# Weights in long contiguous runs, a row-wise MLP and an output tail in four column groups, in a decode block on one core

## Chip, cores, metric

One core of one Trainium2 chip. The metric is device time in microseconds (us) of one execution. "Span" is the time of one profiled execution, about 1.8 us shorter than the device time of the same run.

## The reference, cut

```python
def reference(A_x, A_k_cache, A_v_cache, A_wq, A_wo, B_x, B_w1, B_b1, B_w2, B_b2):
    xn = _layernorm(A_x)                                    # A_x: (8, 1, 640) bf16
    # attention: q = xn @ wq, 32 heads of 128, caches (8, 32, 4096, 128)
    # p = softmax(q k^T / sqrt(128)); o = p v; a = o @ wo    wq (640, 4096), wo (4096, 640)
    # MLP: m = gelu(_layernorm(xn) @ w1 + b1) @ w2 + b2      w1 (640, 1728), w2 (1728, 640)
    return A_x + a + m
```

The two caches are 268 MB each; with the weights the kernel reads 552 MB and does little arithmetic on each byte. This is a streaming problem.

## The kernel before

The caches are cut into 64 tiles (8 batches, 8 groups of 4 heads). A tile is 4.2 MB of K and 4.2 MB of V, with 32 KB runs on each of 128 partitions. There are two K buffers and two V buffers. VectorE computes three quarters of the scores of a tile (two rounds of multiply, add, reduce) and TensorE one quarter (transposes, then matmuls); TensorE multiplies with V.

All loads are issued by SyncE, in the order of a position number, and it waits in that order: a load that may not be issued yet holds back those behind it.

```python
        def kpieces(t):
            return [(0, NJ)]
        ...                                                       # cut
        for t in range(T):
            pos = (-100.0, -94.0)[t] if t < NK else t - 1.5       # K tile t
            ...
            pos = t + 0.6                                         # V tile t
            R = (["wqBfree"], ["wqBfree", "wqAfree", "ovfree"])[t] if t < NV else []
            ...
```

The weights wq and w1 lie in the space of the V buffers until V is loaded. Their rows were spread over partitions as "(c k) n -> k c n", so each partition got five separate rows:

```python
        ld(-99.0, wqa_sb, A_wq[:, 0:QP * P].rearrange("(c k) n -> k c n", k=P), ["wqA"], "wqa")       # 1 KB runs
        ld(-93.0, wqb_sb, A_wq[:, QP * P:H * P].rearrange("(c k) n -> k c n", k=P), ["wqB"], "wqb")   # 7 KB runs
        ld(-95.2, w1_sb, B_w1.rearrange("(c k) f -> k c f", k=P), ["ovw1"], "w1")                     # 3456 B runs
        ld(-95.1, w2_sb[:, 0:FC - 1, :], B_w2[0:(FC - 1) * P, :].rearrange("(c k) n -> k c n", k=P), ["ovw2a"], "w2a")   # 1280 B
```

Only four heads of wq (0.66 MB, 640 KB) are loaded at first, so that the first tiles can start; the other 28 come after K1. The last steps put the output together:

```python
                    for a in range(HT):
                        for k in range(2):
                            r = e.matmul(TRF[0:B, k, 0:D // 2], oTn_sb[:, a, :],
                                         wo_sb[:, a, k * D // 2:(k + 1) * D // 2], start=False, ...)
```

## Time and profile before

| | before |
|---|---|
| device time, first 3 runs | 1297.64 us (1297.46 to 1299.62) |
| span of the profiled run | 1297.0 us |
| bytes moved | 552 MB, mean 426 GB/s |
| VectorE busy | 1119.4 us (86%) |
| VectorE's first multiply starts | 19.15 us |
| last V data landed | 1290.99 us |

First the page of the kernel before: three rows of its 40 equal slices, 32.4 us each. PEclk and DMA are in tenths, GB/s is what the DMA engines moved.

```profile
PEclk9555565555555555555555655556655565555556
DMA  9999999999999999999999999999999999999997
GB/s 383 399 425 433 431 429 434 426 434 432 428 435 425 436 434 428 432 425 436 434 431 431 425 435 435 431 429 431 429 435 431 429 431 429 436 430 426 433 430 302
```

DMA is at 9 (90% or more) in every slice but the last, and from the third slice to the last but one near 430 GB/s. So DMA bounds this kernel, and any change must either move fewer bytes, or touch the two ends.

The chain of waits of the kernel before, from the middle of the run: start, length, what.

```profile
330.16 35.17 DMA KV_sb<-in_A_v_cache_dram
365.38 3.62 PE PV_ps L619 x32
369.01 35.17 DMA KV_sb<-in_A_v_cache_dram
404.22 3.62 PE PV_ps L619 x26
```

The chain alternates between a landing of V (L619 is the product with V, which starts when V is there) and the next issue. The chain goes through every second V tile, so from 365.38 to 404.22 us two K tiles and two V tiles have moved: 16.8 MB in 38.84 us, 432 GB/s. At that rate, 552 MB take 1278 us. The rest, 19 us, is at the ends and in the small loads.

The loads that SyncE issued, in order of time (start, length, engine and line, operation, what; x2 is two merged):

```profile
0.74 0.39 SPq L370 DMA_DIRECT2D KV_sb<-in_A_k_cache_dram  x1
1.19 0.41 SPq L370 DMA_DIRECT2D KV_sb<-in_A_wq_dram  x1
1.65 0.52 SPq L370 DMA_DIRECT2D KV_sb<-in_B_w_dram  x1
2.21 17.41 SPq L370 DMA_DIRECT2D w_sb<-in_B_w_dram  x2
19.67 0.58 SPq L370 DMA_DIRECT2D KV_sb<-in_A_k_cache_dram  x1
20.29 0.43 SPq L370 DMA_DIRECT2D KV_sb<-in_A_wq_dram  x1
...
76.41 0.33 SPq L370 DMA_DIRECT2D KV_sb<-in_A_k_cache_dram  x1
76.78 0.44 SPq L370 DMA_DIRECT2D wo_sb<-in_A_wo_dram  x1
78.02 0.33 SPq L370 DMA_DIRECT2D KV_sb<-in_A_v_cache_dram  x1
93.37 0.33 SPq L370 DMA_DIRECT2D KV_sb<-in_A_k_cache_dram  x1
```

K0, then a part of wq, w1, w2. The two issues of w2 took SyncE 17.4 us (the chain of waits splits them into 8.4 and 9.0), although the view names nothing that they waited for. At 76.41 us K3 was issued, then a wo, V2, and at 93.37 us K4. VectorE's first multiply on a K tile (timeline, VectorE):

```profile
19.15 3.35 DVE L544 TENSOR_TENSOR Y_sb<-KV_sb,qbc_sb 128x6144 bf16<-128x6144 bf16 x1
```

And the end of the chain of waits: the last V piece, the last projection, the output.

```profile
1290.99 0.72 PE PV_ps L629 x32
...
1292.51 2.17 PE TR_ps L669 x8
...
1294.70 0.48 DVE out_sb L749
```

The page's last part gives the median from issue to landing:

```profile
KV_sb<-in_A_k_cache_dram SPq DMA_DIRECT2D x64, 4096.0 KB, 26.8
KV_sb<-in_A_v_cache_dram SPq DMA_DIRECT2D x63, 4096.0 KB, 35.2
```

A V load lands 35.2 us after its issue, but its own transfer is 9.7 us (a quarter of the 38.84 us above): the queue holds more than two loads ahead.

### The profile page before, as it was taken

How to read it: one execution, taken by the hardware profiler on the slowest of the kernel's cores; microseconds unless marked ns; L12 is line 12 of the kernel's file. 1: busy time of each engine (PE TensorE's matmuls, PEld its weight loads, DVE VectorE, ACT ScalarE, POOL GpSimd, SP SyncE). 2: the span in 40 equal slices, each digit the busy share in tenths (PEclk: the TensorE clock that was granted, in tenths of full speed). 3: DMA queues.
4: the chain of work that ended last, by engine and by line, in shares of the span. 5: the costliest groups of instructions: out<-in, count | busy, mean ns of one | idle time of the engine just before them, and what ended most of it. 6: DMA issues, size and time to landing. Idle time of an engine off the chain costs nothing.

```text
span 1297.0 us, 19542 instructions
## 1 busy us (share of the span) xinstructions
PE 657.6 (51%) x7884; PEld 428.4 (33%) x7884; DVE 1119.4 (86%) x574; ACT 493.1 (38%) x1202; POOL 0.2 (0%) x4
## 2 busy tenths in 40 slices
PE   4354554555454455444555445544545544545555
PEld 3233333333233243232333233332332332333332
DVE  7698898898898898888988888988988988988884
ACT  2244344334344244343344343343442443432442
POOL 0000000000000000000000000000000000000000
PEclk9555565555555555555555655556655565555556
DMA  9999999999999999999999999999999999999997
GB/s 383 399 425 433 431 429 434 426 434 432 428 435 425 436 434 428 432 425 436 434 431 431 425 435 435 431 429 431 429 435 431 429 431 429 436 430 426 433 430 302
DMA packets 26738, 552.04 MB, mean 426 GB/s; under 512 B 2313, under 2 KB 8801, under 8 KB 10082
## 3 DMA queue, kind: packets, MB, share of 16 engines
q1 hardware_dynamic: 26688, 551.80, 99.4%
q8 instruction: 10, 0.16, 0.1%
q10 hardware_dynamic: 34, 0.02, 0.0%
q14 instruction: 6, 0.05, 0.0%
HBM read 551.80 MB, written 0.01 MB: 425 GB/s over the span
## 4 chain that ended last, share of the span: by engine, by line
DMA 86%; PE 9%; DVE 2%; SPq 2%; issue 1%; ACT 0%; DVEq 0%
DMA KV_sb<-in_A_v_cache_dram 84%; PE PV_ps L619 8%; DMA KV_sb<-in_A_wq_dram 2%; SPq L370 2%; DVE Y_sb L544 1%; DVE Y_sb L548 0%; PE C_ps L457 0%; PE TR_ps L512 0%; ACT KT_sb L515 0%; PE TR_ps L669 0%; ACT qT_sb L462 0%; ACT S_sb L532 0%; PE PV_ps L629 0%; PE S_ps L522 0%; DVE out_sb L749 0%
## 5 line engine op out<-in xcount | busy, mean ns | idle before, releaser
L544 DVE TENSOR_TENSOR Y_sb<-KV_sb,qbc_sb 128x6144 bf16<-128x6144 bf16 x128 | 429.1, 3352 | 93.9 <-DMA KV_sb<-in_A_k_cache_dram 93.9
L551 DVE TENSOR_REDUCE S_sb<-Y_sb 128x48 f32<-128x3072 bf16 x128 | 429.1, 3353 | 4.4
L515 ACT ACTIVATE KT_sb<-TR_ps 128x1024 bf16<-128x1024 bf16 x256 | 254.8, 1021 | 249.2 <-PE TR_ps L512 247.6
L512 PE MATMUL TR_ps<-ident_bf,KV_sb 128*128 128x128 bf16 x2048 | 249.6, 309 | 102.7 <-DMA KV_sb<-in_A_k_cache_dram 84.2
L619 PE MATMUL PV_ps<-KV_sb,P_sb 128*16 128x512 bf16 x2040 | 224.6, 619 | 130.4 <-DMA KV_sb<-in_A_v_cache_dram 130.4
L512 PEld LDWEIGHTS TR_ps<-ident_bf,KV_sb 128*128 128x128 bf16 x2048 | 201.2, 142 | 115.5 <-DMA KV_sb<-in_A_k_cache_dram 89.2
L548 DVE TENSOR_TENSOR Y_sb<-Y_sb 128x3072 bf16<-128x3072 bf16 x128 | 224.9, 1757 | 4.4
L522 PE MATMUL S_ps<-qk_sb,KT_sb 128*128 128x4 bf16 x2048 | 97.9, 170 | 147.4 <-ACT KT_sb L515 145.8
L638 ACT ACTIVATE E_sb<-PV_ps 128x512 bf16<-128x512 f32 (+1 forms) x65 | 38.5, 592 | 319.8 <-PE PV_ps L619 317.9
L522 PEld LDWEIGHTS S_ps<-qk_sb,KT_sb 128*128 128x128 bf16 x2048 | 86.1, 109 | 178.2 <-ACT KT_sb L515 178.2
L619 PEld LDWEIGHTS PV_ps<-KV_sb,P_sb 128*16 128x16 bf16 x2040 | 63.1, 124 | 242.9 <-DMA KV_sb<-in_A_v_cache_dram 136.0
L583 ACT ACTIVATE P_sb<-S_sb,NB_sb 32x128 bf16<-32x128 f32 x256 | 101.9, 398 | 3.8
L644 PE MATMUL C_ps<-sel_bf,E_sb 128*128 128x4 bf16 x256 | 16.9, 172 | 102.6 <-DVE rinv_sb L600 79.3
L565 PE MATMUL CH_ps<-ident_f,M_sb 128*2 128x128 f32 (+1 forms) x33 | 12.2, 370 | 103.7 <-DVE M_sb L563 103.7
L577 ACT ACTIVATE NB_sb<-CH_ps 128x2 f32<-128x2 f32 (+1 forms) x33 | 5.7, 172 | 152.0 <-PE CH_ps L573 152.0
L532 ACT ACTIVATE S_sb<-S_ps 32x32 f32<-32x32 f32 x256 | 48.2, 188 | 31.5 <-PE S_ps L522 29.2
L644 PEld LDWEIGHTS C_ps<-sel_bf,E_sb 128*128 128x128 bf16 x256 | 11.4, 104 | 134.1 <-DVE rinv_sb L600 79.7
L595 PEld LDWEIGHTS C_ps<-rs_sb,mask_f 128*128 128x128 f32 x256 | 42.7, 252 | 24.1 <-issue 24.1
L583 ACT ACTIVATION_READ_ACCUMULATOR P_sb<-S_sb,NB_sb 32x1 f32 x256 | 47.0, 184 | 0.0
L595 PE MATMUL C_ps<-rs_sb,mask_f 128*128 128x2 f32 x256 | 45.4, 299 | 0.0
L565 PEld LDWEIGHTS CH_ps<-ident_f,M_sb 128*2 128x2 f32 (+1 forms) x33 | 2.6, 80 | 106.6 <-DVE M_sb L563 106.6
L661 DVE TENSOR_TENSOR oTn_sb<-C_ps,rinv_sb 128x8 bf16<-128x8 f32 x32 | 4.7, 147 | 26.8 <-issue 22.5
(82 smaller groups left out, 158.6 us busy)
## 6 DMA issues: line engine op xcount, KB each, us to landing
KV_sb<-in_A_k_cache_dram SPq DMA_DIRECT2D x64, 4096.0 KB, 26.8
KV_sb<-in_A_v_cache_dram SPq DMA_DIRECT2D x63, 4096.0 KB, 35.2
wo_sb<-in_A_wo_dram SPq DMA_DIRECT2D x8, 640.0 KB, 28.0
KV_sb<-in_A_wq_dram SPq DMA_DIRECT2D x1, 4480.0 KB, 28.5
KV_sb<-in_B_w_dram SPq DMA_DIRECT2D x1, 2160.0 KB, 19.2
w_sb<-in_B_w_dram SPq DMA_DIRECT2D x1, 2080.0 KB, 24.3
KV_sb<-in_A_v_cache_dram SPq DMA_DIRECT2D x1, 2048.0 KB, 12.7
KV_sb<-in_A_v_cache_dram SPq DMA_DIRECT2D x2, 1024.0 KB, 15.0
```

Source lines behind the costliest of these rows:

```text
L512: r = e.transpose(TR_ps[:, it.box[0], jj * P:(jj + 1) * P], kv[:, n * BK + jj, :], ident_bf[:, :])
L515: add("act", t - 0.59 + 0.12 * n, lambda e: e.activation(KT_sb[:, m % NS, :, :].rearrange("p a b -> p (a b)"), TR_ps[:, it.box[0], :], ACT ...
L522: r = e.matmul(S_ps[:, c:c + HT], KT_sb[:, m % NS, jj, :], qk_sb[:, :, b % HB], start=True, stop=True)
L532: r = e.activation(S_sb[s, g % SR, i, 0:JP], S_ps[s, 0:JP * HT].rearrange("p (j a) -> p j a", a=HT)[:, :, a], ACT.Copy)
L544: return e.tensor_tensor(y, kv[:, j0:j1, :], qbc_sb[:, g % 2, i, :][:, None, :].to_broadcast([P, nj, P]), ALU.mult)
L548: lambda e, y=y, y2=y2: e.tensor_tensor(y2, y[:, :, 0:P // 2], y[:, :, P // 2:P], ALU.add),
L551: lambda e, y2=y2, j0=j0, j1=j1: e.tensor_reduce(S_sb[:, g % SR, i, j0:j1], y2, AX.X, ALU.add),
L583: r = e.activation(P_sb[s, g % PR, i, :, a, :], S_sb[s, g % SR, i, :].rearrange("p (m c) -> p m c", c=4), ACT.Exp, bias=NB_sb[s, g % 2, i: ...
L595: r = e.matmul(RS_ps[:, a * GT:(a + 1) * GT], mask_f[:, a, :], rs_sb[:, g % PR, :], start=True, stop=True)
L619: r = e.matmul(PV_ps[32 * ct:32 * ct + HT * 4, t % 2, :], P_sb[:, g % PR, i, m, :, :].rearrange("p a c -> p (a c)"), vv[:, 4 * m:4 * m + 4 ...
L638: add("act", pos, lambda e: e.activation(E_sb[:, k, 0:n], PV_ps[:, k, 0:n], ACT.Copy), R=[("PV", k)], W=[("E", k)], X=[("PVb", k)])
L644: r = e.matmul(OT_i, E_sb[:, t % 2, c * P:(c + 1) * P], sel_bf[:, c:HT * 4:4], start=(c == 0), stop=(c == 3 and not last))
```

## The change

It intends to shorten the two ends. The weights get a layout in which each partition holds consecutive rows, so a partition is one contiguous run: 40 KB of wq, 17 KB of w1, 16 KB of w2. The whole wq then comes in one load. The queries and the MLP's hidden layer are computed with activations as rows (8 rows of 512 or 432 columns) and turned by small transposes. TensorE's loop has two tiles instead of four, the row sums take one matmul instead of four, the last sum for the base of the output moves from VectorE to TensorE, and the last projection runs in four column groups side by side.

```diff
-        ld(-99.0, wqa_sb, A_wq[:, 0:QP * P].rearrange("(c k) n -> k c n", k=P), ["wqA"], "wqa")
-        if H > QP:
-            ld(-93.0, wqb_sb, A_wq[:, QP * P:H * P].rearrange("(c k) n -> k c n", k=P), ["wqB"], "wqb")
+        ld(-99.0, wq_sb, A_wq.rearrange("(k c) n -> k c n", c=DC), ["wq"], "wq")
 ... cut
-            pos = (-100.0, -94.0)[t] if t < NK else t - 1.5
+            pos = (-100.0, -98.0)[t] if t < NK else t - 1.5
 ... cut
-            pos = t + 0.6
-            R = (["wqBfree"], ["wqBfree", "wqAfree", "ovfree"])[t] if t < NV else []
+            pos = (0.45, 1.2)[t] if t < NV else t + 0.6
+            R = (["wqfree"], ["wqfree", "w1free", "hfree"])[t] if t < NV else []
 ... cut
-        ld(-95.2, w1_sb, B_w1.rearrange("(c k) f -> k c f", k=P), ["ovw1"], "w1")
-        ld(-95.1, w2_sb[:, 0:FC - 1, :], B_w2[0:(FC - 1) * P, :].rearrange("(c k) n -> k c n", k=P), ["ovw2a"], "w2a")
+        ld(-95.2, w1_sb, B_w1.rearrange("(k c) f -> k c f", c=DC), ["w1"], "w1")
+        ld(-95.1, w2_sb[:, 0:FC, :], B_w2[0:FC * P, :].rearrange("(k c) n -> k c n", c=FC), ["w2"], "w2")
 ... cut: row queries and row MLP
+            for n in range(H * P // 512):       # 8 blocks of 512 columns
+                        for kc in range(DC):
+                            i = e.matmul(TRF[0:B, it.box[0], :], xnT_sb[:, 0, kc, :], wq_sb[:, kc, s],
+                                         start=(kc == 0), stop=(kc == DC - 1))
 ... cut: row sums
-                for a in range(HT):
-                    r = e.matmul(RS_ps[:, a * GT:(a + 1) * GT], mask_f[:, a, :], rs_sb[:, g % PR, :],
-                                 start=True, stop=True)
+            add("pe", rp, lambda e: e.matmul(RS_ps, ones_f[:, :], rs_sb[:, :, :].rearrange("p a g -> p (a g)"),
+                                             start=True, stop=True),
 ... cut: last projection
-                        for k in range(2):
-                            r = e.matmul(TRF[0:B, k, 0:D // 2], oTn_sb[:, a, :],
-                                         wo_sb[:, a, k * D // 2:(k + 1) * D // 2], start=False,
+                        for k in range(4):
+                            r = e.matmul(TRF[32 * k:32 * k + B, 0, 0:D // 4], oTn_sb[:, a, :],
+                                         wo_sb[:, a, k * D // 4:(k + 1) * D // 4], start=False,
```

## The prediction

> What bounds it now. The DMA queue. The page's slices show the 16 engines 99% busy from the third slice to the last but one, at about 431 GB/s; the chain of waits is 84% landings of V tiles. The Trainium skill ("DMA: Bandwidth & Descriptors", section "Where 436 GB/s comes from") gives a fabric ceiling of 435 GB/s, and the trace agrees: in the middle of the run a K tile and a V tile (8.39 MB) land every 38.85 us, 432 GB/s. All 552 MB at 432 GB/s are 1278 us of the 1297 us span. Only 19 us are not at this rate: about 2 us before data flow, a poor stretch in the first 64 us (windows of 4 us: 293 GB/s at 12 to 16 us, 262 at 56 to 60 us), 8 loads of wo (1.75 us each where 1.5 is the full rate), thinning out over the last 5 us, and 6.0 us from the last V landing (1291.0) to the end. VectorE is second: a tile takes 17.0 us, a pair with its softmax 36.8 us (from 64.6 to 101.4 us, timeline), against 38.85 us of DMA.
>
> What changes.
> 1. Longer runs for wq, w1, w2. From the DMA records (an estimate from packet sizes and durations), 1 KB packets move 19.4 B/ns per engine, 1280 B 22.3, 3456 B 24.6, 7 KB 25.9, 32 KB 26.9. At 26.9 the weights (9.7 MB) cost 2.5 us less of all-engine time. This removes the poor stretch at 12 to 16 us, and the issue that sat 17 us on w2.
> 2. But the whole wq (5.2 MB) must land before any query, where 0.64 MB did. Before, VectorE's first multiply started at 19.2 us. Now: K0 and wq land at about 24 us; 40 matmuls of 512 columns, some 9 to 12 us (0.43 us each at half clock, from four concurrent PV matmuls taking 0.43; half that before the throttle, which came some 7 us after PE got busy); 32 small transposes, 2 to 3 us; copies and broadcast 1.7 us. First multiply at about 38 us. Loads queued ahead (wq, K1, w1, w2, V0) keep DMA busy to about 54 us. K2 and V1 should be just in time, but K4 waits for VectorE's last multiply of tile 2, about 48 us after its first multiply: 86 us, when the queue has run dry at 83. I expect a hole of about 4 us there, and after 108 us as many bytes moved as before, within 1 MB. Then VectorE catches up by 1 us a tile.
> 3. Row MLP, row sums in one matmul, two-tile loop, qbc in its own bank: save PE time, which is off the path. Steady state stays 38.85 us a pair.
> 4. Tail: the last projection, 8 matmuls of 320 columns in sequence (2.15 us), becomes 16 of 160 in four column groups, about 0.6 to 0.8 us; outputs in halves cost about the same. Minus 1.4 us, all on the path.
>
> Sum: 1297.6 - 1.4 (tail) - 0.5 (start, -2.5 and the better queue against the hole) = 1295.7 us, range 1290.5 to 1300.5. Faster by over 2%: 0.01; within 2%: 0.98; slower by over 2%: 0.01.
>
> Right if: pair period unchanged at 38.85; first multiply at 36 to 41 us; DMA low in some window between 82 and 90 us; last landing to end 4.4 to 5.0 us.
>
> Wrong if: the queries run faster, or K4's hole is filled (then up to 5 us better); the MLP on PE frees V1 late, or PE is throttled through the queries, VectorE starting at 46 us (up to 8 us worse); or the steady rate shifts.

## The result, and the profile after

| | before | after |
|---|---|---|
| device time, 4 runs each | 1298.63 us (1297.46 to 1301.33) | 1297.93 us (1297.65 to 1299.02) |
| span of the profiled run | 1297.0 us | 1296.1 us |
| VectorE's first multiply | 19.15 us | 39.09 us |
| last V data landed | 1290.99 us | 1290.96 us |
| from there to the end | 6.0 us | 5.1 us |

The ratio is 0.9993, with a 95% interval of 0.9975 to 1.0011: the same. A ratio is the mean time of one kernel's fast runs over that of the other's in the same rounds, so it is not quite the ratio of the medians above.

A large rewrite thus moved the last landing by 0.03 us; below it turns out that two larger terms cancelled there. The page of the kernel after, same rows:

```profile
PEclk9655556555565555556555555555665556655566
DMA  9989999999999999999999999999999999999997
GB/s 405 426 360 431 430 435 430 428 430 432 434 431 430 427 435 434 429 432 425 437 433 428 434 425 436 433 427 436 425 435 432 429 435 426 434 432 428 432 430 330
```

The first two slices are better (405 and 426 against 383 and 399 GB/s). The third is worse: 360 against 425. What was won in 65 us was given back in the next 32, and somewhat more. Part of the gain is not run length: the kernel before had a low place of its own at 56 to 60 us (262 GB/s; 395 after), where V0 was issued only at 56.29 us, when the queries of the other 28 heads had freed the space of wq. The windows of 4 us around that place in the kernel after (busy us of each engine with counts in brackets, granted clock, DMA share, GB/s):

```profile
80.00:84.00 4.00, 1.61 (x28) 1.61 (x29) 3.96 (x3) 3.54 (x10) 0.00 (x0) 0.50 0.85 363
84.00:88.00 4.00, 3.26 (x43) 1.72 (x45) 3.96 (x2) 2.48 (x6) 0.00 (x0) 0.50 0.02 4
88.00:92.00 4.00, 2.24 (x21) 0.80 (x10) 3.96 (x2) 0.60 (x1) 0.00 (x0) 0.50 1.08 393
```

From 84 to 88 us DMA moved 4 GB/s. Windows of 1 us put the hole from 83.3 us (131 GB/s in the 84th us) to 88.0 us: 4.7 us. In the kernel before, the same three windows have 459, 414 and 418 GB/s. The loads that SyncE issued in the kernel after:

```profile
0.74 0.41 SPq L365 DMA_DIRECT2D KV_sb<-in_A_k_cache_dram  x1
1.20 0.41 SPq L365 DMA_DIRECT2D KV_sb<-in_A_wq_dram  x1
1.66 0.42 SPq L365 DMA_DIRECT2D KV_sb<-in_A_k_cache_dram  x1
2.13 0.50 SPq L365 DMA_DIRECT2D KV_sb<-in_B_w_dram  x1
2.67 1.11 SPq L365 DMA_DIRECT2D w_sb<-in_B_w_dram  x2
...
87.30 0.36 SPq L365 DMA_DIRECT2D KV_sb<-in_A_k_cache_dram  x1
89.90 0.34 SPq L365 DMA_DIRECT2D KV_sb<-in_A_v_cache_dram  x1
```

The whole set of weights was now issued by 3.8 us, without the 17 us. But K4 was issued at 87.30 us only, and V2 at 89.90, after 2.0 us more of waiting for the product with V0 to free its buffer. K4 needs the buffer of K2, and VectorE read K2 until 87 us. It was late because it had started late (timeline of the kernel after):

```profile
25.18 10.81 PE L451 MATMUL TR_ps<-KV_sb,xnT_sb 128*8 128x512 bf16 x40 [12.51 <-DMA KV_sb<-in_A_wq_dram]
27.51 0.59 ACT L455 ACTIVATE Y_sb<-TR_ps 8x512 bf16<-8x512 f32 x1 [16.08 <-PE TR_ps L451]
29.55 0.59 ACT L455 ACTIVATE Y_sb<-TR_ps 8x512 bf16<-8x512 f32 x1 [1.45 <-PE TR_ps L451]
30.62 0.59 ACT L455 ACTIVATE Y_sb<-TR_ps 8x512 bf16<-8x512 f32 x1 [0.49 <-PE TR_ps L451]
...
39.09 3.36 DVE L543 TENSOR_TENSOR Y_sb<-KV_sb,qbc_sb 128x6144 bf16<-128x6144 bf16 x1 [25.49 <-ACT qbc_sb L482]
...
83.67 3.35 DVE L543 TENSOR_TENSOR Y_sb<-KV_sb,qbc_sb 128x6144 bf16<-128x6144 bf16 x1
```

wq landed at 25.18 us; the 40 matmuls of the queries took 10.81 us; VectorE started at 39.09. Before, it started at 19.15. The last line is its last multiply on K2: it ends at 87.02, and K4 is issued 0.3 us later.

The copies of the query blocks also show how fast TensorE was: they start at 27.51, 29.55, 30.62 us and then every 1.08 us. The first two blocks (ten matmuls) took about 2.1 us each, 0.43 us per matmul of 512 columns, the others 0.215. The Trainium skill, "TensorE: Matmul & The Clock Gate", Part 1, says that an idle TensorE runs at half rate until about 3.4 us of sustained work have passed; this trace agrees: the rate changed at 29.3 us, 4.1 us after the first of these matmuls.

The steady state of the kernel after, same view as before:

```profile
331.56 35.17 DMA KV_sb<-in_A_v_cache_dram
366.77 3.62 PE PV_ps L615 x29
370.41 35.19 DMA KV_sb<-in_A_v_cache_dram
405.63 3.62 PE PV_ps L615 x30
```

366.77 to 405.63 us is 38.86 us, against 38.84. And the end:

```profile
1290.96 1.12 PE PV_ps L625 x32
...
1292.89 0.73 PE TR_ps L664 x16
...
1293.65 0.31 DVE out_sb L766
```

The last projection took 0.73 us instead of 2.17. The last product with V (L625, L629 before) took 1.12 us instead of 0.72 though; it is the same work at a lower granted clock (the 2 us window from 1290 us on reads 0.50 after, 1.00 before).

The start cost more than the 0.03 us between the last landings show. Summed in windows of 20 us, the kernel after had moved 1.6 MB more than the kernel before at 80 us and 0.7 MB less at 100 us, and it stayed 0.4 to 0.8 MB behind up to 1280 us: on average 0.54 MB, which is 1.25 us at 432 GB/s. It caught up only in the last 10 us of the transfers. The windows there, two of the kernel before and then the same two of the kernel after (the last two numbers are DMA share and GB/s):

```profile
1286.00:1288.00 2.00, 1.41 (x20) 1.27 (x24) 0.21 (x1) 0.53 (x1) 0.00 (x0) 1.00 0.71 291
1288.00:1290.00 2.00, 1.29 (x28) 0.36 (x16) 0.00 (x0) 0.60 (x1) 0.00 (x0) 1.00 0.19 78
1286.00:1288.00 2.00, 1.04 (x16) 0.31 (x16) 0.15 (x1) 0.00 (x0) 0.00 (x0) 1.00 1.02 426
1288.00:1290.00 2.00, 0.80 (x8) 0.11 (x8) 0.00 (x0) 0.60 (x1) 0.00 (x0) 0.70 0.54 217
```

In the kernel before, part of the DMA engines already had nothing left to do from 1286 us on, while the last data landed at 1290.99 all the same. In the kernel after they were full up to 1288 us. Why is open, and there is only one trace of the kernel before. That the two last landings agree is therefore luck: the start lost 1.25 us and the end of the transfers gave it back.

### The profile page after: what moved, and what is told of

Its sections match the earlier page's. It is cut to its first block, busy times and chain, and to the rows that moved or that the text cites. A ratio compares the mean times of both kernels' runs of the same rounds, so it can differ in the third digit from the quotient of the medians.

```text
span 1296.1 us, 19692 instructions
## 1 busy us (share of the span) xinstructions
PE 650.0 (50%) x7853; PEld 408.1 (31%) x7853; DVE 1121.7 (87%) x586; ACT 500.3 (39%) x1241; POOL 0.2 (0%) x4
## 4 chain that ended last, share of the span: by engine, by line
DMA 77%; DVE 10%; PE 9%; issue 3%; ACT 0%; SPq 0%; DVEq 0%
DMA KV_sb<-in_A_v_cache_dram 75%; PE PV_ps L615 7%; DVE Y_sb L543 5%; DVE Y_sb L547 3%; DVE S_sb L550 2%; DMA KV_sb<-in_A_wq_dram 2%; PE TR_ps L451 1%; PE CH_ps L564 0%; DVE M_sb L562 0%; SPq L365 0%; PE PV_ps L625 0%; PE PV_ps L689 0%; PE TR_ps L462 0%; DVE rinv_sb L596 0%; PE TR_ps L664 0%
## 5 line engine op out<-in xcount | busy, mean ns | idle before, releaser
L566 DVE TENSOR_REDUCE M_sb<-CH_ps 2x4 f32<-2x128 f32 (+1 forms) x33 | 9.2, 279 | 15.9 <-PE CH_ps L564 15.9
L675 PE MATMUL ACC_ps<-oTn_sb,wo_sb 128*128 128x8 bf16 x620 | 21.5, 169 | 0.0
## 6 DMA issues: line engine op xcount, KB each, us to landing
w_sb<-in_B_w_dram SPq DMA_DIRECT2D x1, 2080.0 KB, 43.8
```

The source lines that it names most:

```text
L675: r = e.matmul(ACC_ps[:, c * B:(c + 1) * B], wo_sb[:, a, c * P:(c + 1) * P], oTn_sb[:, a, :], start=False, stop=False, skip_group_check=True)
```

## The experiments

My theory: the long runs do save DMA time, but the start is paced by VectorE's first multiply, which now waits for the whole wq and all queries. Two K buffers let VectorE's lateness through to the queue at K4; the queue runs dry at 83.3 us, and everything after K4 is shifted. The rivals: the longer runs give nothing; or all DMA time counts and the change has simply added as much as it removed; or TensorE's work matters.

The runs were made in three calls, on different chips. The kernel before had medians of 1298.32, 1300.77 and 1299.13 us. The new code varied less: the kernel after had 1297.93 and 1298.44. Differences of half a us between runs therefore say little, and the landings in the traces are compared as well as the times. Every result was correct.

### wq_first: wq before K0

```diff
-        ld(-99.0, wq_sb, ...)
+        ld(-100.5, wq_sb, ...)        # K0 is at -100.0
```

> The changed kernel, with only the order of the first two loads turned: wq, then K0. Theory (the gain of the long runs is lost in a hole before K4, because VectorE starts 39.1 us into the span, after the whole wq and the queries): wq lands 9.7 us earlier, VectorE's first multiply comes at about 29.4 us, K4 is issued at about 77.6 us, before the queue runs dry at 83.3 us, so the hole of 4.7 us (83.3 to 88.0 us) is gone and the time falls by 4 to 5 us, to about 1293.3 us, with the steady pair still at 38.85 us. Rival (the longer runs simply give nothing, the first stage is bound by bytes and small costs, and the hole would only move elsewhere): within 1 us of 1297.9 us.

Measured: 1293.18 us (1292.96 to 1293.26, 5 runs), the kernel before beside it 1298.32; ratio 0.9961 (0.9947 to 0.9974). VectorE's first multiply at 30.25 us, last landing at 1285.99. The window in which the hole was, in this run:

```profile
84.00:88.00 4.00, 1.89 (x16) 1.62 (x16) 2.04 (x1) 0.95 (x2) 0.00 (x0) 0.50 0.99 426
```

The hole is gone (K4 was issued at 78.60), and with it 4.75 us of time and 4.97 us at the last landing. The same bytes, the same packets, the same instructions on every engine but SyncE: only two loads changed places. This version beats both kernels, by 0.4%; under the 2% line that still counts as the same.

### wq_third: wq after K1

```diff
-        ld(-99.0, wq_sb, ...)
+        ld(-97.0, wq_sb, ...)         # K1 is at -98.0
```

> The changed kernel with wq after K1 instead of before it. Theory (startup is paced by VectorE's first multiply): first multiply 9.7 us later, at about 48.8 us, K4 issued at about 97 us, all later loads 9.7 us later, time about 1307.6 us. Rival (the DMA queue has slack for this, the total is bytes over rate): no change, 1297.9 us.

Measured: 1307.51 us (1307.15 to 1308.14). First multiply at 48.56 us, 9.47 us later than in the kernel after; time 9.58 us more. One us of start costs one us of total. The rival, that the queue has slack, falls. The time was lost in other places, though: with the queries later, V0 and K2 were issued later too (45.48 and 60.39), and the queue ran low from 44 to 48 us (151 GB/s) and from 56 to 64 us (41 and 250 GB/s) already.

### k4_parts: only K4 in three pieces

```diff
         def kpieces(t):
-            return [(0, NJ)]
+            return [(32, 80), (0, 32), (80, NJ)] if t == 4 else [(0, NJ)]
```

> The changed kernel with the load of K tile 4 alone in three pieces, columns 32 to 80 first, so that a piece can be issued when VectorE's first multiply of tile 2 is over (78.6 us) instead of its second (87.3 us). The loops of the engines then start a few tiles later; the order of operations is the same. Theory: the hole at 83.3 to 88.0 us closes, but K5 is still issued at 104.2 us and the queue now runs dry at about 102.8 us: a new hole of 2 to 3 us there, so the time falls by only about 2 us, to 1296. Rival (a hole is a hole: filling it gives it all back): 4.7 us less, 1293.2. Rival (the hole is unimportant): 1297.9.

Measured: 1295.54 us (1294.97 to 1295.67), 2.4 us less than the kernel after; last landing at 1288.71, 2.25 us earlier. The windows of this run:

```profile
84.00:88.00 4.00, 3.26 (x44) 1.77 (x43) 3.97 (x2) 2.67 (x6) 0.00 (x0) 0.50 0.96 401
...
100.00:104.00 4.00, 2.92 (x32) 0.80 (x24) 4.00 (x2) 0.60 (x1) 0.00 (x0) 0.50 0.80 340
104.00:108.00 4.00, 0.00 (x0) 0.00 (x0) 3.93 (x3) 0.00 (x0) 0.00 (x0) 0.50 0.78 262
```

The hole at 84 us is filled, and a smaller one stands at 100 to 108 us, where 340 and 262 GB/s replace 430: (430 - 340 + 430 - 262) x 4 / 430 = 2.4 us lost. Half of what was filled came back as the next wait, as expected: K5 was still issued at 104.21 us.

### k4to7_parts: K4 to K7 in three pieces

```diff
-            return [(0, NJ)]
+            return [(32, 80), (0, 32), (80, NJ)] if 4 <= t < 8 else [(0, NJ)]
```

> As k4_parts, for K tiles 4 to 7. Theory: K5 and K6 are issued before the queue runs dry too, no hole from 83 us to 130 us, 4 to 5 us less than the changed kernel, about 1293.3 us, although VectorE's first multiply stays at 39.1 us. If VectorE itself bounded the first stage, it would stay at 1296 to 1298.

Measured: 1294.94 us (1293.92 to 1294.98), 3.0 us less than the kernel after, last landing at 1287.63, 3.3 us earlier; its first multiply was at 39.49 us. (The profiled run, 1293.92 us, was the fastest of the five.) The two places where the holes stood:

```profile
84.00:88.00 4.00, 3.26 (x49) 1.98 (x50) 3.96 (x3) 2.81 (x6) 0.00 (x0) 0.50 1.00 418
...
100.00:104.00 4.00, 3.12 (x32) 0.92 (x24) 4.00 (x2) 0.76 (x2) 0.00 (x0) 0.50 0.92 392
```

No 4 us window between 80 and 140 us is below 385 GB/s, so the holes are gone while VectorE's start stayed late. I had expected 4 to 5 us. Part of the rest is the pieces themselves: their packets of 8 and 12 KB moved at 26.1 and 26.3 B/ns per engine against 26.9 for 32 KB, which is about 0.9 us more by the packet durations (512 packets x 9.4 ns and 1024 x 10.1 ns, over 16 engines). The remaining half us I have not followed up.

### short_runs: the packets of before, in the kernel after

```diff
-        ld(-99.0, wq_sb, A_wq.rearrange("(k c) n -> k c n", c=DC), ["wq"], "wq")
+        for a, (n0, n1) in enumerate([(0, 512), (512, H * P)]):
+            ld(-99.0 + 0.01 * a, wq_sb[:, :, n0:n1], A_wq.rearrange(...)[:, :, n0:n1], [("wq", a)], "wq")
+        # w1: one load for each c, 3456 B runs; w2: one load for each c, 1280 B runs
```

> The changed kernel with the packets of the kernel before: wq in 1 KB and 7 KB runs (two loads), w1 in five loads of 3456 B runs, w2 in thirteen of 1280 B runs; same bytes into the same places. The short runs cost about 2.5 us more of all-engine time (from the packet durations: wq 1.0, w1 0.5, w2 1.0). Theory (VectorE paces the start through wq): only wq's part counts, since wq lands 1.0 us later and K4 is issued 1.0 us later; the 1.5 us of w1 and w2 are swallowed by the hole, which shrinks. Time about 1299.0, plus 1.0 us. Rival (every us of DMA time counts): plus 2.5 us, 1300.4. Rival (run length means nothing here): 1297.9.

Measured: 1300.08 us (1299.44 to 1300.73); the kernel before 1300.77. Last landing at 1293.77, 2.81 us later than in the kernel after. First multiply at 41.84, 2.75 us later. So the whole loss again equals the delay of VectorE's start, as the theory says; but my size for it, 1.0 us, was wrong, and on the time alone the rival (2.5 us) did better. wq landed 1.9 us later, not 1.0. By 28 us the DMA had moved 0.3 MB less than in the kernel after by the 4 us windows, 0.4 MB by the packet records, which is 0.7 to 1.0 us at 432 GB/s: no more than the packet durations had said. Why the last piece of wq landed later still was not followed up. The queries took 11.64 us instead of 10.81. This run could not part the theories.

### wq_first_short: the same, without a hole

```diff
 # short_runs, and
-            ld(-99.0 + 0.01 * a, wq_sb[:, :, n0:n1], ...)
+            ld(-100.5 + 0.01 * a, wq_sb[:, :, n0:n1], ...)
```

> As short_runs, on top of wq_first, where there is no hole. Theory: now every us of DMA time counts, so the short runs cost the whole 2.5 us: 1295.7 against 1293.2. Rival (only wq's landing counts, here too): plus 1.0 us, 1294.2.

Measured: 1295.91 us (1295.28 to 1296.11), 2.7 us above wq_first; last landing 3.1 us later, while the first multiply was only 2.1 us later (32.36 against 30.25). SyncE was busy issuing w2 up to 42.86 us, so that V0 was issued at 42.90 instead of 27.18; but no 4 us window from 4 to 92 us is below 347 GB/s, so the queue did not run dry over it. Here more was lost than VectorE's delay: without a hole DMA itself counts.

### short_w1_w2 and wq_first_short_w1_w2: short runs only where wq is not touched

```diff
-        ld(-95.2, w1_sb, B_w1.rearrange("(k c) f -> k c f", c=DC), ["w1"], "w1")
+        for c in range(DC):
+            ld(-95.2 + 0.001 * c, w1_sb[:, c, :], B_w1.rearrange("(k c) f -> k c f", c=DC)[:, c, :], [("w1", c)], "w1")
         # w2 likewise; wq in 40 KB runs, at -99.0 (first) or -100.5 (second kernel)
```

> The changed kernel with wq in long runs, and w1 and w2 alone in the short runs of the kernel before (3456 B and 1280 B). They cost about 1.5 us of all-engine time after wq has landed. Theory (VectorE, started by wq, paces the loads up to K4, and the hole before K4 has room): VectorE's first multiply at 39.1 us as in the changed kernel, hole 1 to 1.5 us shorter at its front, time unchanged within 0.5 us of the changed kernel. Rival (every us of DMA time counts): plus 1.5 us.

> The same short w1 and w2 on top of wq_first, where there is no hole. Theory: here every us of DMA time counts: plus 1.0 to 1.5 us against wq_first's 1293.2, so 1294.2 to 1294.7. Rival (w1 and w2 never matter): 1293.2.

Beside them on the same chip, the kernel after once more:

> The changed kernel itself once more, to stand beside the next two on the same chip (the kernel before ran 1297.6 to 1301.9 us within the last call): 1297.9, within 1 us.

Measured: after_again 1298.44 us (1297.95 to 1298.73), short_w1_w2 1297.97 us (1297.28 to 1298.87), wq_first_short_w1_w2 1293.96 us (1293.91 to 1294.11). In the kernel after, the short runs of w1 and w2 cost nothing: the times overlap, and the last landing moved by 0.44 us with a first multiply 0.34 us later (39.83 against 39.49). The window from 80 to 84 us moved 459 GB/s instead of 369, since the queue ran dry later: the hole took them in. In wq_first they cost 0.8 us of time and 1.0 us of landing, a little less than expected; wq_first itself was timed in another call. So the long runs of w1 and w2 save something like 0.8 us where no hole follows, and the kernel after cannot collect it.

### old_tail: the last projection and output copies as before

```diff
-                        for k in range(4):
-                            r = e.matmul(TRF[32 * k:32 * k + B, 0, 0:D // 4], oTn_sb[:, a, :], ...
+                        for k in range(2):
+                            r = e.matmul(TRF[0:B, k, 0:D // 2], oTn_sb[:, a, :], ...
         # the base likewise in two parts; one copy of 320 columns on each engine
```

> The changed kernel with the last projection as before: two parts of 320 columns one after the other on the same rows, and the output written by one copy on each engine. Theory (the tail is all on the path): from the last V landing to the end about 6.3 us in place of 5.1, at the same clock (projection 2.15 in place of 0.71, copies 0.48 in place of 0.64), so plus 1.2 us, 1299.1. Rival (the gain of the change in the tail was luck of the clock): within 0.3 us of 1297.9.

Measured: 1299.85 us (1298.75 to 1300.19), against 1297.93 and 1298.44 for the kernel after, and 1298.09 for rowsum_x4 below, which has the new tail. In the trace, from the last landing (1291.47) to the end of the span (1298.1) 6.6 us, against 5.1: the projection took 2.30 us instead of 0.71, the copies 0.48 instead of 0.64. The last product with V took 1.06 us busy in both. At the same clock the new tail is worth 1.5 us; it showed 0.9 between the two profiled runs, since that product ran in 0.65 us before.

### rowsum_x4: the row-sum matmul four times

```diff
-            add("pe", rp, lambda e: e.matmul(RS_ps, ones_f[:, :], rs_sb[...], start=True, stop=True),
+            def pe_rs(e):
+                for _ in range(4):
+                    r = e.matmul(RS_ps, ones_f[:, :], rs_sb[...], start=True, stop=True)
+                return r
+            add("pe", rp, pe_rs,
```

> The changed kernel with the row-sum matmul issued four times for each group (same result each time), which adds more matmul time to TensorE than the one-matmul row sum saved: 96 more float32 matmuls of about 0.6 us. Theory (TensorE is off the path except in the tail): no change in the steady state, pair at 38.85 us; in the last group at most a few tenths of a us; 1297.9 within 0.5. Rival (TensorE time counts): up to tens of us more.

Measured: 1298.09 us (1297.49 to 1298.73). The group's busy time on TensorE rose from 16.1 to 45.6 us, as much as the four masked matmuls had before (45.4), and nothing came of it. What the change saves on TensorE in the steady state is off the path.

## Why the prediction was right, point by point

- **DMA bounds, and the steady pair stays.** 38.84 us before, 38.86 after. Right. One wording in the text is wrong: in 38.85 us not one K tile and one V tile (8.39 MB) land, but two of each, 16.8 MB; only that gives the 432 GB/s that stand there, and the sums built on it.
- **First multiply at about 38 us.** 39.09. Right; the queries' 10.8 us lie within the 9 to 12 predicted. The reason given for their speed was not: I expected full clock first and half clock later; the first two blocks ran at half rate and the rest at full rate.
- **Queue dry at 83 us, K4 at 86, a hole of about 4 us.** Dry at 83.3, K4 at 87.30, hole 4.7 us. Right, and shown: wq_first removes it and 4.75 us of time (1297.93 to 1293.18).
- **"After 108 us as many bytes moved as before, within 1 MB".** Summing the 4 us windows gives 43.3 MB after and 43.8 before. Right.
- **Start worth 0.5 us.** Wrong in sign. By the bytes moved, the start cost about 1.25 us: up to 80 us 1.6 MB (3.75 us at 432 GB/s) were won, between 80 and 100 us 2.3 MB (5.3 us) were lost. The hole was 0.7 us longer than expected, and the windows beside it (363 and 393 GB/s) stayed below the full rate too. The last landing moved by 0.03 us only because the end of the transfers, which the prediction left as it was, happened to give the same amount back.
- **Tail minus 1.4 us.** Minus 0.9 between the profiled runs. The projection saved 1.44 us as costed; a product with V just ahead of it ran at half clock and took 0.4 us back, and two output copies cost 0.16 us more than one.
- **Last landing to end, 4.4 to 5.0 us.** 5.1, just outside; the product at half clock makes 0.4 of it.
- **In total minus 1.9 us.** The medians differ by 0.7 us, the interval of the ratio includes no change at all. The range held, with some luck in the term of the start.
- **Long runs worth 2.5 us.** Put together by wq_first and wq_first_short: 2.7 us in time, 3.1 in landing. Right in sum. The split over the weights was wrong: w1 and w2 gave 0.8 to 1.0 instead of 1.5, wq gave the larger part. Each figure is good to about half a us.

Where the expected gain went: it was there (by the 4 us windows, 34.9 MB had moved by 84 us, against 33.7 in the kernel before), and it was given back, with 1.25 us on top, around one wait, because the same edit that made wq one long run also put 5.2 MB and ten us of matmuls ahead of VectorE's first work. Before, 0.66 MB of wq in 1 KB runs started VectorE 20 us earlier. That this split had been paying for itself is argued from this; no run puts it into the new code.

Open: why the granted clock at the end was 0.5 in all but one of the runs with the new code (k4to7_parts ran the last product with V in 0.65 us), the last half us of k4to7_parts, and why the DMA engines end more nearly together in the kernel after.

## What to carry to other kernels

In a kernel bound by DMA, judge a change in the first stage by when the slowest consumer starts and when its first buffers come free again, not only by the bytes saved: the loss shows several tiles later, as a load issued after the queue has run dry. Load first what the consumer's longest preparation needs (here wq, whose queries take 11 us, before K0, which is not touched until they are done); on top of this rewrite, exchanging two loads brought 4.75 us where the rewrite alone had brought less than one. When a hole is found, try filling it alone: if half comes back as the next hole, the consumer's start is the cause, not that one load.

## What the Trainium skill lacked or had wrong

- "DMA: Bandwidth & Descriptors", section "Why small descriptors are slow (HBM only)": about 3 cycles of overhead per packet. For 1280 B that is 40 beats of 32 B and 3 cycles, an estimate from that page of 7%; the 32 B of descriptor data that it also counts would make it 9%. Measured from the packets of these traces: 22.3 B/ns per engine for 1280 B, 26.9 for 32 KB, 27.05 for 40 KB, so 17% less. The page has no table by run length for loads issued by SyncE; here 1 KB gave 19.4, 3456 B 24.6, 7 KB 25.9 B/ns.
- The same page, section "Issuing engines are not separate DMA queues", calls the sequencer's time to initiate a DMA usually small. With many short runs in the queue it was not: the two issues of w2 in 1280 B runs took 8.4 and 9.0 us in the kernel before, and 1.1 us together in long runs, and the loads behind them had to wait for SyncE. It is not the load's own runs that count: the second of these two issues has only 64 of them, and in short_runs the issue of K1, in its usual 128 runs of 32 KB, took 7.81 us behind the short runs of wq, against 0.42 us in the kernel after. Waiting for room behind what was queued before would fit; no run tested it.
- The same page, section "Where 436 GB/s comes from": a ceiling of 435 GB/s; the steady state here reaches 432. It agrees. The same section says that between HBM and SBUF the HBM side, about 358 GB/s, binds instead; with one core running, these loads were well above that.
- "TensorE: Matmul & The Clock Gate", Part 1: agrees on the half-rate start (0.43 us, then 0.215 us per matmul of 512 columns). The views print a granted clock of 1.00 from 25 to 36 us, but the trace holds no clock record before 29.28 us, where its first one (1.00) begins and the matmuls become fast. So the 1.00 before that is not a measurement, and the start has to be read from the spacing of the matmuls.
